# Linear-attention layer and MLP on one core: both tiles of a pair combined in one visit, the second in two of the MLP's banks

## The chip, the core and the metric

The kernel runs on one core of one Trainium2 chip. A core has five engines that each run their own list of instructions in order: TensorE (PE, matrix products; its weight loads are listed as PEld), VectorE (DVE), ScalarE (ACT), GpSimd (POOL) and SyncE (SP, which here issues most transfers). Semaphores order the lists against each other. Matrix products are written to PSUM, a small memory of eight banks per partition; DVE and ACT read them from there. The metric is the time of one execution on the device in microseconds (us).

## The reference

Input x is 2048 tokens of 576 numbers in bf16. The first half is attention with feature maps and no attention matrix; the second half is an MLP. Both have a residual.

```python
def A(x, wqkv, w_phi, wo):                    # 32 heads of 18
    q, k, v = split(x @ wqkv)
    pq, pk = q @ w_phi, k @ w_phi             # per head, 18 x 18
    phi_q = concat(softmax(pq), softmax(-pq)) # 36 features
    phi_k = concat(softmax(pk), softmax(-pk))
    kv, z = phi_k.T @ v, phi_k.sum(tokens)    # 36 x 18 and 36, per head
    o = (phi_q @ kv) / (phi_q @ z + 1e-6)
    return o @ wo

def B(x, w1, b1, w2, b2):                     # 576 -> 4608 -> 576
    return gelu(layernorm(x) @ w1 + b1) @ w2 + b2

h  = x + A(layernorm(x), ...)
h2 = h + B(layernorm(h), ...)
```

## The kernel before

The 2048 tokens are 16 tiles of 128 (NT = 16), taken in eight pairs of 256 (TB). Tile t belongs to pair p = t // 2.

The prologue normalises x, makes keys and values for all pairs and sums phi_k.T @ v over all tokens into `acc_kv`. It also makes the exponentials of the queries of all pairs, which wait in SBUF. From the masked table `kvm` on, each tile needs only its own queries. Pair 0 is finished there, with steps of its own.

The rest is the MLP, and the attention of the later pairs is threaded through it. `first_block` runs the MLP for pair 0, `second_block` for pair 1, and `double_block` for pairs 2 and 3, then 4 and 5, then 6 and 7.

- `up` (L1129) is the first layer. It has 18 steps, which the text calls pairs of `up`, numbered 0 to 17: in each, 18 matmuls (L1142) fill two banks `ph`, which ACT reads and writes as gelu to a buffer (L1164). The matmuls use 64 of the 128 rows of the array each (64 of 576 inputs at a time), two in turn on the two halves. One pair of tiles gives 256 columns, a double block 512.
- `down` (L1170) is the second layer. A tile's output is two `po` tiles of 288 columns, each the sum of 36 matmuls with all 128 rows (L1186). They are numbered from 0 through the block by k: 144 in a block of one pair, 288 in a double block. DVE adds `hb` (residual and bias, made by POOL at L1175) and writes `ot` (L1190), which SP sends out.

Both take a dictionary `at`: at a given step of `up`, or before a given matmul k of `down`, a piece of the attention is called. All engines are under a manual schedule, so each engine runs its instructions in the order in which the program calls them: where a piece stands in `at` is where it stands on every engine.

The pieces for a pair p are:

- `norm_q(p, i)`: DVE sums one half of the exponentials and takes the reciprocal (`query_sum`, L503 and L504); POOL multiplies them into `padded` (`query_weigh`, L512 and L522).
- `turn_q(p)`: two transposing transfers on SP turn `padded` into `phiT[p]` (L546). Most pairs use the buffer `phit`; pairs 3 and 5 take two of the eleven SBUF buffers called homes. The home of the pair's exponentials is given back here. Homes are taken from the front of a list and given back to its end; the gelu outputs of `up` live in homes too.
- `combine(t)` (L664): `combine_mm` multiplies the tile's queries with `kvm` in eleven matmuls of 57 or 38 columns (L641) into a tile `pn` of two banks; `divide` then divides by the denominators on DVE, in four instructions (L654 twice, L655 twice), into `ob`. `pn_pool` holds one tile, so the matmuls of the next `combine` wait until the last `divide` has read it.
- `leave(p)`: `combine` of the odd tile, then `turn(p)`, a transposing transfer of `ob` on SP (L672).
- `enter(p)`: the products with `wo` (L689), the residual (L698), the second layernorm and its transposes (L735), ahead of the MLP for that pair.

After the prologue PSUM is divided so: two banks for `pn_pool`, and six for the pool `acc`, from which `ph`, `po` and the products `pa` of `enter` take one bank at a time:

```python
    acc = ctx.enter_context(
        tc.tile_pool(name="acc", bufs=6, space=bass.MemoryType.PSUM, reuse_waits="tile")
    )
```

`combine` of the even tile is called by itself, before `leave` of the pair:

| Block | even tiles (`combine`) | odd tiles (`leave`) |
|---|---|---|
| first, `down` | tile 2 at 0, tile 4 at 84 | pair 1 at 12, pair 2 at 118 |
| second, `up` | tile 6 at step 10 | pair 3 at step 12 |
| second, `down` | tile 8 at 98, tile 10 at 122 | pair 4 at 110, pair 5 at 136 |
| double (pairs 2 and 3), `down` | tile 12 at 110, tile 14 at 190 | pair 6 at 130, pair 7 at 210 |

Of the kernel before, what the change touches and what calls it, by code (L numbers as in the profile page):

```python
# [8 lines left out]
P = 128  # L9
BF16 = mybir.dt.bfloat16  # L10
FP32 = mybir.dt.float32
# [16 lines left out]
VW = DH + 1  # L28
# [15 lines left out]
def kernel(  # L44
# [39 lines left out]
    def take(key):  # L84
        taken[key] = vacant.pop(0)
        return homes[taken[key]][:, :]

    def leave_home(key):
        vacant.append(taken.pop(key))
# [3 lines left out]
    kvm = persist.tile([P, KW, WV], BF16, name="kvm", tag="kvm")  # L93
# [11 lines left out]
    pn_pool = ctx.enter_context(  # L105
        tc.tile_pool(name="pn_pool", bufs=1, space=bass.MemoryType.PSUM, reuse_waits="tile")
    )
    psA = ctx.enter_context(ExitStack())
    two = psA.enter_context(
        tc.tile_pool(name="two", bufs=3, space=bass.MemoryType.PSUM, reuse_waits="tile")  # L110
    )
# [26 lines left out]
    def region(at, n):  # L138
        return shared[:, at : at + n]
# [314 lines left out]
    phik, phiq, phiT = {}, {}, {}  # L454
# [44 lines left out]
    def query_sum(p, i):  # L499
        if p not in rescaled:  # L500
            rescaled[p] = small.tile([P, 2, 2 * NH], FP32, name="rq", tag="rq", bufs=3)
        sk = small.tile([P, 2, NH], FP32, name="sk", tag="sk", bufs=6)
        nc.vector.tensor_reduce(sk[:, :, :], part_of(phiq[p], i), AX.X, ALU.add)  # L503
        nc.vector.reciprocal(rescaled[p][:, :, i * NH : (i + 1) * NH], sk[:, :, :])  # L504

    def query_weigh(p, part, a, eng):
        src = phiq[p][:, a, :].rearrange("p (h f) -> p h f", f=DH)
        rk = rescaled[p][:, a, :]
        n = 2 * WH
        g0 = part * 5  # L510
        hs = slice(g0 * n, (g0 + 5) * n)
        eng.tensor_tensor(  # L512
            padded[:, a, g0 * P : (g0 + 5) * P].rearrange("p (g k) -> p g k", k=P)[
                :, :, 0:STEP
            ].rearrange("p g (h f) -> p g h f", f=DH),
            src[:, hs, :].rearrange("p (g h) f -> p g h f", h=n),
            rk[:, hs].rearrange("p (g h o) -> p g h o", h=n, o=1).to_broadcast([P, 5, n, DH]),
            ALU.mult,
        )
        if part:  # L520
            m = 2 * COUNT[-1]
            eng.tensor_tensor(  # L522
                padded[:, a, KW * P - m * DH : KW * P].rearrange("p (h f) -> p h f", f=DH),
                src[:, 2 * NH - m :, :],
                rk[:, 2 * NH - m :].rearrange("p (h o) -> p h o", o=1).to_broadcast([P, m, DH]),
                ALU.mult,
            )

    def norm_q(p, i):
        query_sum(p, i)  # L530
        for a in range(2):
            query_weigh(p, i, a, pool)

    def turn_q(p):
        if p == 0:
            whole = region(4 * PW, 2 * KW * P).rearrange("p (a w k) -> p a w k", a=2, k=P)
            phiT[p] = [whole[:, a, :, :] for a in range(2)]
        elif p in (3, 5):
            phiT[p] = [
                take(("phiT", p, a))[:, 0 : KW * P].rearrange("p (w k) -> p w k", k=P)  # L540
                for a in range(2)
            ]
        else:
            phiT[p] = [phit[:, a, :, :] for a in range(2)]
        for a in range(2):
            nc.sync.dma_start_transpose(phiT[p][a], padded[:, a, :])  # L546
        leave_home(("phiq", p))

    left = list(range(NT))

# [78 lines left out]
    products = {}  # L629

    def combine_mm(t, part=None, home=None):
        p, a = divmod(t, 2)
        if not part:
            products[t] = (home or pn_pool).tile(
                [P, 2, 512], FP32, name="pn", tag="two" if home else "pn"
            )
        pn = products[t]
        for w in range(*((0, KW) if part is None else BANKS[part])):
            b = w // 6
            at, n = (w - BANKS[b][0]) * WV, COUNT[w] * VW  # L640
            nc.tensor.matmul(  # L641
                pn[:, b, at : at + n], phiT[p][a][:, w, :], kvm[:, w, 0:n],
                start=True, stop=True,
            )
        if part != 0 and ("phiT", p, a) in taken:
            leave_home(("phiT", p, a))

    def divide(t):
        o = ob[t // 2 % 2][:, :, t % 2, :].rearrange("p c (e h) -> p c e h", e=2)
        rec = small.tile([P, NH], FP32, name="rec", tag="rec")  # L650
        for w0, w1_ in BANKS:
            h0, h1 = FIRST[w0], min(NH, w1_ * WH)
            pv = products[t][:, w0 // 6, 0 : (h1 - h0) * VW].rearrange("p (h v) -> p h v", v=VW)
            nc.vector.reciprocal(rec[:, h0:h1], pv[:, :, DH])  # L654
            nc.vector.tensor_tensor(  # L655
                o[:, :, :, h0:h1],
                pv[:, :, 0:DH].rearrange("p h (c e) -> p c e h", e=2),
                rec[:, h0:h1].rearrange("p (u v h) -> p u v h", u=1, v=1).to_broadcast(
                    [P, KC, 2, h1 - h0]
                ),  # L660
                ALU.mult,
            )

    def combine(t):  # L664
        combine_mm(t)
        divide(t)

    def out_rows(p):
        return ob[p % 2][:, :, :, :].rearrange("p c a k -> p (c a k)")
# [1 line left out]
    def turn(p):  # L671
        nc.sync.dma_start_transpose(oT[p % 2][:, :, :], out_rows(p))  # L672
# [41 lines left out]
    def residual(p, banks):  # L714
        for i in range(2):
            residual_mm(p, i, banks())
            for a in range(2):
                residual_add(p, i, a)
            for a in range(2):
                residual_stats(p, i, a)  # L720
                if i:
                    second(2 * p + a)

    def rescale(t, half):
        mv, rs = moved[t]
        normalise(ln2[t % 2][:, :, half, :], chunks(t), mv, rs, 0)
# [7 lines left out]
    def turn2(t):  # L734
        nc.sync.dma_start_transpose(place2(t), rows2(t))  # L735

    def turn2_mm(t, home=None):
        transposes(("2", t), rows2(t), home)
# [18 lines left out]
    def close_weights():  # L757
# [362 lines left out]
    acc = ctx.enter_context(  # L1120
        tc.tile_pool(name="acc", bufs=6, space=bass.MemoryType.PSUM, reuse_waits="tile")
    )
# [75 lines left out]
    def enter(a):  # L1198
        residual(a, two_banks)
        for t in (2 * a, 2 * a + 1):  # L1200
            rescale(t, 0)
            rescale(t, 1)
            turn2(t)

    def leave(p, following=None):
        combine(2 * p + 1)
        if following:
            turn_q(following)
        turn(p)
# [4 lines left out]
    def first_block():  # L1214
        rise = up(0, 1, {}, 1)
        turn2_mm(1, pn_pool)
        next(rise)
        for n in range(2):
            load_w2(1, n)
        for part in range(2):  # L1220
            turn2_ev(1, part, dve)
        for q in (1, 2):
            for i in range(2):
                norm_q(q, i)
            if q == 1:
                turn_q(q)
                for n in range(2, 6):
                    load_w2(1, n)
        down(0, 1, next(rise), {
            0: lambda: combine(2), 12: lambda: (leave(1), turn_q(2)), 66: lambda: enter(1),  # L1230
            84: lambda: combine(4),
            96: lambda: norm_q(3, 0), 118: lambda: leave(2),
        })

    def second_block():
        hidden = next(up(1, 1, {
            3: lambda: (norm_q(3, 1), turn_q(3)),
            6: lambda: norm_q(4, 0),
            8: lambda: (norm_q(4, 1), turn_q(4)),
            10: lambda: combine(6),  # L1240
            12: lambda: leave(3),
            14: lambda: norm_q(5, 0),
            16: lambda: (norm_q(5, 1), turn_q(5)),
        }))
        enter(2)
        down(1, 1, hidden, {
            44: lambda: enter(3), 98: lambda: combine(8), 110: lambda: leave(4),
            122: lambda: combine(10), 136: lambda: leave(5),
        })

    def double_block(p):
        rises, falls = {}, {}
        if p == 2:
            rises = {
                3: lambda: norm_q(6, 0), 6: lambda: (norm_q(6, 1), turn_q(6)),
                12: lambda: norm_q(7, 0), 15: lambda: norm_q(7, 1),
            }
            falls = {
                110: lambda: combine(12), 130: lambda: leave(6, 7),
                190: lambda: combine(14), 210: lambda: leave(7),  # L1260
            }
        hidden = next(up(p, 2, rises))
        if p + 2 < NS:
            enter(p + 2)
            enter(p + 3)
        down(p, 2, hidden, falls)
# [36 lines left out]
```

## Time and profile before

| What | Before |
|---|---|
| median of 3 runs | 393.16 us (392.96 to 394.19) |
| the profiled execution's own time | 392.96 us |
| its span | 391.2 us |
| PE / DVE / ACT / POOL busy | 98% / 42% / 42% / 33% of the span |
| `po` matmuls (L1186) | 144.0 us busy, 1151 recorded |
| `ph` matmuls (L1142) | 141.5 us busy, 1638 |
| `divide`: L654 and L655 | 8.1 us in 32 and 14.6 us in 32 instructions |

The span is the time from the first to the last recorded work of the profiled execution; its own time is a little longer. In the lines below, the chain in order of time has the start, the length, and what the time went to; "issue" is time in which an engine waited for nothing that the profile shows. A row of the timeline has the start, the length, the engine, the line and the operation, output and inputs, and in brackets how long the engine stood idle before and what ended that. Rows that say x11 take eleven instructions together. Matmuls overlap, so the length of a group in the timeline is a little more than its share of the chain.

### The profile page before, as it was taken

What the parts mean: (1) busy time and instruction counts of PE and PEld (TensorE: products, weight loads), DVE (VectorE), ACT (ScalarE), POOL (GpSimd) and SP (SyncE); (2) the same over time, 40 slices, a digit from 0 to 9 for tenths busy, and PEclk for the clock granted to TensorE, in tenths of its full rate; (3) what the DMA queues carried; (4) which work ended last, traced back from release to release, by engine and by line L of the source; (5) the groups of instructions that cost most, each with busy time, mean ns of one, the idle gap of its engine ahead of it and who ended that gap; (6) DMA issues with size and microseconds to landing.
All of it is one profiled execution on the core that took longest, in us unless ns stands there. A gap on an engine that the chain in (4) does not pass through costs nothing.

```text
span 391.2 us, 10255 instructions
## 1 busy us (share of the span) xinstructions
PE 383.5 (98%) x4492; PEld 266.6 (68%) x4493; DVE 164.2 (42%) x367; ACT 163.5 (42%) x290; POOL 128.2 (33%) x167
## 2 busy tenths in 40 slices
PE   8899999999999999999999999999999999999997
PEld 4687777779878887744457887444677764447773
DVE  6988893694259478680029431000480000000100
ACT  4978878688401850046650000666300016661000
POOL 8999998215514563144003111000031110000120
PEclk9999999999999999999999999999999999999999
DMA  8999749999455466532004532000041000000000
GB/s 224 197 169 168 173 107 202 230 315 251 159 106 122 76 107 134 107 78 45 0 2 63 124 72 47 17 1 2 2 104 48 17 17 0 2 2 0 17 28 19
DMA packets 76108, 34.76 MB, mean 89 GB/s; under 512 B 63026, under 2 KB 73536, under 8 KB 76064
## 3 DMA queue, kind: packets, MB, share of 16 engines
q1 hardware_dynamic: 75376, 32.47, 39.9%
q0 software_dynamic: 400, 1.35, 1.3%
q8 instruction: 35, 0.57, 0.6%
q10 hardware_dynamic: 288, 0.30, 0.2%
q14 instruction: 9, 0.07, 0.1%
HBM read 16.53 MB, written 2.36 MB: 48 GB/s over the span
## 4 chain that ended last, share of the span: by engine, by line
PE 94%; DVE 4%; POOL 1%; issue 1%; POOLq 0%
PE po L1186 36%; PE ph L1142 36%; PE pk L426 7%; PE pa L689 5%; PE pv L426 4%; PE acc_kv L559 2%; PE pn L641 1%; PE pw L250 1%; DVE st L293 1%; POOL wv L174 1%; DVE ob L655 0%; PE pW L396 0%; DVE shared L260 0%; PE pT L338 0%; DVE shared L314 0%
## 5 line engine op out<-in xcount | busy, mean ns | idle before, releaser
L1164 ACT ACTIVATE home<-ph,b1col 128x512 bf16<-128x512 f32 (+1 forms) x180 | 98.5, 598 | 170.7 <-PE ph L1142 167.4
L1186 PE MATMUL po<-w,home 128*128 128x288 bf16 (+2 forms) x1151 | 144.0, 286 | 0.1
L1142 PE MATMUL ph<-shared,w 64*128 64x512 bf16 (+2 forms) x1638 | 141.5, 331 | 0.1
L1186 PEld LDWEIGHTS <-home 128*128 128x128 bf16 x1152 | 109.0, 98 | 31.7 <-issue 1.6
L1142 PEld LDWEIGHTS <-w 64*128 64x128 bf16 x1638 | 80.1, 94 | 60.2 <-issue 1.2
L1190 DVE TENSOR_TENSOR ot<-po,hb 128x288 bf16<-128x288 f32 (+2 forms) x32 | 14.5, 454 | 108.3 <-PE po L1186 104.8
L1175 POOL TENSOR_TENSOR hb<-xh,b2bc 128x576 f32<-128x576 bf16 x16 | 20.4, 1272 | 103.6 <-DVE ot L1190 94.3
L426 PEld LDWEIGHTS <-home 64*128 64x128 bf16 x864 | 41.9, 94 | 10.6 <-issue 0.9
L512 POOL TENSOR_TENSOR padded<-home,rq 128x540 bf16<-128x540 bf16 x32 | 34.8, 1102 | 35.2 <-DVE rq L504 14.5
L256 POOL TENSOR_TENSOR rs<-va,mhalf 128x1 f32<-128x1 f32 x16 | 8.8, 550 | 108.3 <-DVE va L254 108.3
L698 DVE TENSOR_TENSOR xh<-pa,xh 128x288 bf16<-128x288 f32 x32 | 13.2, 450 | 73.7 <-PE pa L689 73.7
L483 POOL TENSOR_TENSOR phik<-phik,rk 128x576 bf16<-128x576 bf16 x32 | 36.3, 1160 | 1.1 <-DVE rk L479 0.8
L477 DVE TENSOR_REDUCE sk<-phik 128x64 f32<-128x1152 bf16 x16 | 21.2, 1327 | 4.8 <-ACT phik L448 4.8
L448 ACT ACTIVATE home<-pk 128x576 bf16<-128x576 f32 x32 | 18.9, 650 | 6.7 <-PE pk L426 5.5
L503 DVE TENSOR_REDUCE sk<-home 128x64 f32<-128x1152 bf16 x16 | 21.0, 1313 | 0.0
L426 PE MATMUL pv<-wv,home 64*128 64x288 bf16 x288 | 20.8, 283 | 0.1
L448 ACT ACTIVATE phik<-pk 128x576 bf16<-128x576 f32 x32 | 18.7, 652 | 3.1 <-PE pk L426 3.1
L426 PE MATMUL pk<-wqp,home 64*128 64x288 bf16 x288 | 19.8, 283 | 0.2 <-ACT home L448 0.2
L426 PE MATMUL pk<-shared,home 64*128 64x288 bf16 x288 | 19.8, 283 | 0.0
L689 PE MATMUL pa<-wo,shared 64*128 64x288 bf16 x288 | 18.8, 283 | 0.0
L654 DVE RECIPROCAL rec<-pn 128x18 f32<-128x18 f32 (+1 forms) x32 | 8.1, 252 | 24.6 <-PE pn L641 24.6
L689 PEld LDWEIGHTS <-shared 64*128 64x128 bf16 x288 | 13.8, 94 | 4.4 <-issue 0.5
(78 smaller groups left out, 209.9 us busy)
## 6 DMA issues: line engine op xcount, KB each, us to landing
w<-in_B_w_dram SPq DMA_DIRECT2D x21, 432.0 KB, 7.5
out_dram<-ot SPq DMA_DIRECT2D x15, 144.0 KB, 1.9
xh<-in_A_x_dram SPq DMA_DIRECT2D x3, 576.0 KB, 6.8
wo<-in_A_wo_dram SPq DMA_DIRECT2D x4, 324.0 KB, 7.0
w<-in_B_w_dram POOLq DMA_DIRECT2D x3, 432.0 KB, 10.3
wv<-in_A_wqkv_dram SPq DMA_DIRECT2D x2, 324.0 KB, 9.0
w<-in_A_wqkv_dram SPq DMA_DIRECT2D x4, 157.5 KB, 8.8
wqp<-wqp SPq DMA_DIRECT2D x2, 288.0 KB, 4.0
```

Of the source, the lines that this page charges most:

```text
L426: nc.tensor.matmul(dst[:, a, 0:HALF], lhs[rows, c, :], w[rows, slot, i * HALF : (i + 1) * HALF], start=(n == 0), stop=(n == KC - 1),)
L448: nc.scalar.activation(rows[:, :, i * HH : (i + 1) * HH, s, :], flight[key, p, i][:, :, 0:HALF].rearrange("p a (h f) -> p a h f", f=DH), A ...
L477: nc.vector.tensor_reduce(sk[:, :, :], part_of(dst, i), AX.X, ALU.add)
L483: eng.tensor_tensor(part, part, flight["r" + key, p, i][:, a, :].rearrange("p (h o) -> p h o", o=1).to_broadcast([P, NH, DH]), ALU.mult,)
L503: nc.vector.tensor_reduce(sk[:, :, :], part_of(phiq[p], i), AX.X, ALU.add)
L512: eng.tensor_tensor(padded[:, a, g0 * P : (g0 + 5) * P].rearrange("p (g k) -> p g k", k=P)[:, :, 0:STEP].rearrange("p g (h f) -> p g h f", ...
L689: nc.tensor.matmul(pa[a], oT[p % 2][rows, c, :], wo[rows, c, cs], start=(c == 0), stop=(c == KC - 1),)
L1142: nc.tensor.matmul(ph[half][:, lo:hi], w1[p_ // 9][rows, c, p_ % 9 * P : (p_ % 9 + 1) * P], ln2T[rows, c, base + lo : base + hi], start=(c ...
L1164: nc.scalar.activation(hidden(m), ph[half][:, 0:width], AF.Gelu_apprx_tanh, bias=b1col[:, m : m + 1], scale=1.0,)
L1175: nc.gpsimd.tensor_tensor(hb[:, :], xh[:, t, :], b2bc[:, :], ALU.add)
L1186: nc.tensor.matmul(po[:, :], hidden(m)[:, i_ * P : (i_ + 1) * P], w2[m // 18][:, m % 18, cs], start=(j == 0), stop=(j == NM - 1),)
L1190: nc.vector.tensor_tensor(ot[:, cs], po[:, :], hb[:, cs], ALU.add)
```

## The change

`leave(p)` now does both tiles: the products of the even tile into `pn_pool`'s tile, those of the odd tile into two tiles of one bank each from `acc` (`acc_banks`), and then both divisions, the even tile's first. The separate calls of `combine` are gone, and some of the places in `at` are moved: the visit of pair 1 is at matmul 2, of pair 2 at 112, of pair 4 at 104; pairs 3, 5, 6 and 7 stay where `leave` was. `products[t]` becomes a list of two banks, so that the code of both kinds of tile is the same. The home of a pair's exponentials is given back at the end of `norm_q(p, 1)`, when POOL has been told to weigh them, and no longer in `turn_q` (pair 0 excepted).

```diff
@@ norm_q
         query_sum(p, i)
         for a in range(2):
             query_weigh(p, i, a, pool)
+        if i:
+            leave_home(("phiq", p))
@@ turn_q
             nc.sync.dma_start_transpose(phiT[p][a], padded[:, a, :])
-        leave_home(("phiq", p))
+        if p == 0:
+            leave_home(("phiq", p))
@@ combine_mm
         if not part:
-            products[t] = (home or pn_pool).tile(
-                [P, 2, 512], FP32, name="pn", tag="two" if home else "pn"
-            )
+            if home is acc_banks:
+                products[t] = home()
+            else:
+                whole = (home or pn_pool).tile(
+                    [P, 2, 512], FP32, name="pn", tag="two" if home else "pn"
+                )
+                products[t] = [whole[:, b, :] for b in range(2)]
...
-                pn[:, b, at : at + n], phiT[p][a][:, w, :], kvm[:, w, 0:n],
+                pn[b][:, at : at + n], phiT[p][a][:, w, :], kvm[:, w, 0:n],
...
-    def combine(t):
-        combine_mm(t)
-        divide(t)
+    def acc_banks():
+        return [
+            acc.tile([P, 512], FP32, name="pn", tag="acc")[:, :] for _ in range(2)
+        ]
...
     def leave(p, following=None):
-        combine(2 * p + 1)
+        combine_mm(2 * p)
+        combine_mm(2 * p + 1, None, acc_banks)
+        divide(2 * p)
+        divide(2 * p + 1)
         if following:
             turn_q(following)
         turn(p)
@@ first_block
-            0: lambda: combine(2), 12: lambda: (leave(1), turn_q(2)), 66: lambda: enter(1),
-            84: lambda: combine(4),
-            96: lambda: norm_q(3, 0), 118: lambda: leave(2),
+            2: lambda: (leave(1), turn_q(2)), 66: lambda: enter(1),
+            96: lambda: norm_q(3, 0), 112: lambda: leave(2),
@@ second_block
-            10: lambda: combine(6),
             12: lambda: leave(3),
...
-            44: lambda: enter(3), 98: lambda: combine(8), 110: lambda: leave(4),
-            122: lambda: combine(10), 136: lambda: leave(5),
+            44: lambda: enter(3), 104: lambda: leave(4), 136: lambda: leave(5),
@@ double_block
-                110: lambda: combine(12), 130: lambda: leave(6, 7),
-                190: lambda: combine(14), 210: lambda: leave(7),
+                130: lambda: leave(6, 7), 210: lambda: leave(7),
```

More of the change, by code (lines that the diff above doesn't have):

```diff
@@ L652, in divide @@
             h0, h1 = FIRST[w0], min(NH, w1_ * WH)
-            pv = products[t][:, w0 // 6, 0 : (h1 - h0) * VW].rearrange("p (h v) -> p h v", v=VW)
+            pv = products[t][w0 // 6][:, 0 : (h1 - h0) * VW].rearrange("p (h v) -> p h v", v=VW)
             nc.vector.reciprocal(rec[:, h0:h1], pv[:, :, DH])
```

## The prediction

> **What bounds the kernel now.** I read the page first: engine shares, clock, shares of the chain that ended last.
>
> ```profile
> span 391.2 us, 10255 instructions
> PE 383.5 (98%) x4492; PEld 266.6 (68%) x4493; DVE 164.2 (42%) x367; ACT 163.5 (42%) x290; POOL 128.2 (33%) x167
> ...
> PEclk9999999999999999999999999999999999999999
> ...
> PE 94%; DVE 4%; POOL 1%; issue 1%; POOLq 0%
> ```
>
> TensorE is busy 98% of the span at the full granted clock and makes 94% of the chain; so a change is worth what it takes off TensorE's own stream. Next I read the chain in order of time around each visit of the combining products (L641). The first answer holds the visits of the first block's second layer, at matmuls 0, 12, 84 and 118:
>
> ```profile
> 102.38 0.42 PE pn L641 x11
> 102.79 1.48 PE po L1186 x12
> 104.27 0.11 issue
> 104.38 0.47 PE pn L641 x11
> 104.85 6.62 PE po L1186 x54
> ...
> 116.10 0.31 PE pn L641 x11
> ...
> 120.58 0.31 PE pn L641 x11
> ```
>
> The second holds the second block: tiles 6 and 7 among the pairs of `up`, tiles 8 to 11 in `down` at 98, 110, 122 and 136:
>
> ```profile
> 134.01 0.41 PE pn L641 x11
> 134.42 2.07 PE ph L1142 x36
> 136.49 0.41 PE pn L641 x11
> 136.91 6.00 PE ph L1142 x108
> ...
> 159.64 0.31 PE pn L641 x11
> 159.95 1.48 PE po L1186 x12
> 161.43 0.11 issue
> 161.54 0.47 PE pn L641 x11
> 162.01 1.48 PE po L1186 x12
> 163.49 0.12 issue
> 163.60 0.47 PE pn L641 x11
> 164.07 1.72 PE po L1186 x14
> 165.79 0.34 PE pn L641 x11
> ```
>
> The third holds the double block, tiles 12 to 15, first and last of four equal visits:
>
> ```profile
> 220.18 0.31 PE pn L641 x11
> ...
> 233.37 0.31 PE pn L641 x11
> ```
>
> An undisturbed visit between `po` matmuls costs 0.31 us. Three cost 0.58: 0.11 or 0.12 of idle time, then 0.47, because the weight load could not run ahead of the wait. What they wait for is in the timeline, a waiting pair of tiles first and an unhurried one behind it:
>
> ```profile
> 103.82 0.42 DVE L655 TENSOR_TENSOR ob<-pn,rec 128x252 bf16<-128x252 f32 x1
> 104.35 0.39 PEld L641 LDWEIGHTS <-phit 128*128 128x128 bf16 x11 [0.39 <-issue]
> ...
> 160.97 0.42 DVE L655 TENSOR_TENSOR ob<-pn,rec 128x252 bf16<-128x252 f32 x1
> 161.51 0.39 PEld L641 LDWEIGHTS <-phit 128*128 128x128 bf16 x11 [0.39 <-issue]
> ...
> 221.51 0.42 DVE L655 TENSOR_TENSOR ob<-pn,rec 128x252 bf16<-128x252 f32 x1
> 222.66 0.48 PEld L641 LDWEIGHTS <-phit 128*128 128x128 bf16 x11
> ```
>
> The weight load starts 0.11 and 0.12 us behind the end of the previous tile's last division (104.24, 161.39): with one `pn` tile, the next tile's products wait until the last one is divided. Twelve `po` matmuls (1.48) are too short a distance. At 222.66 the division had ended 0.73 us before, and nothing waited.
>
> **The change, part by part.**
>
> *The distance-12 waits go.* The odd tile's products no longer need the pool's only tile. Matmuls 0 and 12 become one visit at 2: 0.42+0.11+0.47 = 1.00 becomes 0.31+0.31, and the step from the row-split `ph` to `po`, which no row shows alone; its bounds are 0 and the 0.11 by which a `pn` visit next to `ph` (0.42) exceeds one next to `po` (0.31). I take 0.08, as the exit from `ph` is only part of that row: saved 0.30, at least 0.27, at most 0.38. Visits 98, 110, 122, 136 become 104 and 136: 0.31+0.58+0.59+0.34 = 1.82 becomes 1.24: saved 0.58.
>
> *Visits without a wait merge at no gain.* Matmuls 84 and 118 (now 112), and 110, 130, 190, 210 (now 130, 210): six at 0.31 become three at 0.62, since the second eleven matmuls still run. Saved 0, between -0.05 and +0.05 by the rounding of the rows.
>
> *In `up`, one of two excursions goes.* Leaving `ph` and coming back costs more than a visit in `po`: 0.41 against 0.31, and the 36 `ph` matmuls between the two visits took 2.07 where 6.00/108 gives 2.00. Two excursions (0.41 twice, 0.07 beside) become one with 0.31 more: saved 0.10 to 0.17; I take 0.14.
>
> *A new wait: two of six banks are out while DVE divides.* In the second layer that is free: a `po` tile takes 36 x 6.62/54 = 4.4 us and needs one bank, and the four divisions of a tile take 1.32 (next fence, 118.79 to 120.11), so a pair takes about 2.64. The even tile is divided first. In `up` it is tight:
>
> ```profile
> 118.79 0.27 DVE L654 RECIPROCAL rec<-pn 128x18 f32<-128x18 f32 x1
> ...
> 120.11 1.34 DVE L503 TENSOR_REDUCE sk<-home 128x64 f32<-128x1152 bf16 x1
> ...
> 133.94 0.48 PE L641 MATMUL pn<-kvm,home 128*128 128x57 bf16 x11
> ...
> 134.46 0.27 DVE L654 RECIPROCAL rec<-pn 128x18 f32<-128x18 f32 x1 [4.44 <-PE pn L641]
> 134.77 0.50 DVE L655 TENSOR_TENSOR ob<-pn,rec 128x324 bf16<-128x324 f32 x1
> ```
>
> As the changed kernel is built, tile 7's two banks, before pair 12, are pair 9's; they go on to the first half of pair 14 and the first half of pair 15. Count from the visit's first matmul. The first division starts at 0.52 (133.94 to 134.46); tile 7's begins at 0.52+1.32 = 1.84; its first bank is read by 1.84+0.81 = 2.65 (134.46 to 135.27), and TensorE sees that 0.12 later, at 2.77; the second bank at 0.52+2.64+0.12 = 3.28. TensorE is through tile 6 at 0.31, tile 7 at 0.72, and two pairs of 18 x 6.00/108 = 1.00 bring it to pair 14 at 2.72, its weight load a little earlier. It stalls some 0.05 to 0.12, and as in the waits above the halted weight load adds 0.16 (0.47 less 0.31): 0.21 to 0.28. If the load is not caught, 0. I take 0.23, as the sum decides for a late load by little. Pair 15 comes at 3.9, behind its bank's 3.28: no second stall. DVE was idle 4.44 us before the division (row 134.46), so nothing is queued ahead of it.
>
> *Waits on ScalarE.* Tile 3's products now need two banks of `ph` pairs 15 and 16, whose activations are the fifth- and fourth-last of this row:
>
> ```profile
> 85.75 17.48 ACT L1164 ACTIVATE home<-ph,b1col 128x256 bf16<-128x256 f32 x36 [0.41 <-PE ph L1142]
> ...
> 137.25 3.86 SPq L546 DMA_TRANSPOSE phit<-padded  x2
> ...
> 141.20 1.31 SPq L672 DMA_TRANSPOSE shared<-ob  x1
> 141.77 1.10 POOL L512 TENSOR_TENSOR padded<-home,rq 128x540 bf16<-128x540 bf16 x1 [3.22 <-DMA phit<-padded]
> ```
>
> At 17.48/36 = 0.486 each they end at 103.23 - 4 x 0.486 = 101.29 and at 101.77; tile 3's products start at about 103. Cost 0.
>
> *What is queued behind the longer divisions.* On DVE the `ot` addition (L1190) after a visit comes up to 1.3 us later; its bank is not asked for again for several `po` tiles, and `hb` on POOL has 4.4 us. In `up` the query sums of pair 5 stand behind it and come up to 1.3 later, but POOL's weighing, their reader, stood 3.22 us for a DMA until 141.77; cost 0, and if that cover went, 1.3 on POOL, which no TensorE row near it waits for. On SP, `turn(3)` waits for the last division, now about 133.94 + 2 x 1.00 + 3.28 = 139.2; it already stood behind the transposes of `turn_q(4)` (row 137.25) until 141.20. In `down` of the first block the visit at 112 lies 32 matmuls ahead of `up`, whose pair 1 takes the first of its banks: it comes 0.62 + 32 x 6.62/54 + 1.00 = 5.5 behind the visit's start, and the bank is free at 2.77, or with a whole query sum (1.34) ahead of the divisions at 4.1. Cost 0.
>
> *Queries' buffers given up when weighed.* `leave_home` moves ahead of the two `take`s in `turn_q`, but freed homes go to the end of the list; as built, ACT, POOL and SP have the same instructions, homes and order as before. So the transposes that a visit issues (`turn`, `turn_q`) pass no other transfer in SP's queue; those of the first visit, ten matmuls earlier, only start sooner. Cost and gain 0.
>
> **Sum.** 0.30+0.58+0+0.14-0.23 = 0.79 us saved; with the ends, 0.27+0.58-0.05+0.10-0.28 = 0.62 to 0.38+0.58+0.05+0.17 = 1.18. The profiled execution took 392.96 (span 391.2 and 1.76 around it) and would take 392.17. The median of the runs stands 0.20 above it; from there, 393.16 - 0.79 = 392.37. I give 392.3, between the two.
>
> **Rivals.**
> - *All the waits go and no bank is missed*: 1.0 to 1.18 saved, 392.0 to 392.15. For it: TensorE reaches pair 14 within 0.1 us of the bank's release, and one late weight load decides. Against it: by the row 134.46 it is the division that comes last.
> - *The bank wait eats the gain*: pair 14 waits for the whole visit's divisions, 0.56 after it is ready (3.28 less 2.72), with 0.16 for the load 0.72, and pair 15 and the activations behind it fall out of step for a pair's half (0.5): 1.22 lost against 1.02 saved, 393.4, no change. For it: six banks hold only three pairs. Against: each bank has its own wait. The Trainium skill (Perfetto Trace Analysis, section Optimization Strategy) reads a gap that recurs on the busiest engine as a possible shortage of PSUM for the next tile. By that rule the loan of two banks in `up` makes a new shortage, and the time would be 393.4 where the rows of the divisions give 392.3; the trace agrees with it for the gaps of 0.11, which end when the one `pn` tile is divided, and shows none yet for the banks of `up`.
> - *Slower*: the divisions of the visit in `up` start late. Each us for which DVE is held there goes straight to TensorE at pair 14; the gain is gone from 0.79 us of delay, and the time is 0.3% above the median from 1.97. With one query sum ahead (1.34) it is 392.37 + 1.34 = 393.7, with two 395.0. For it: such sums are called four pairs before and two pairs behind the visit. Against: DVE had idled 4.44 us when the visit came two pairs earlier (row 134.46).
>
> **How the numbers follow.** Likeliest 0.62 (391.8 to 392.6), no bank missed 0.18, eaten 0.10, slower 0.10. Of 393.16, 0.3% is 1.18 us, about what a measurement of this kernel can tell from no change: only the top of the first rival and the runs' own spread reach it, so faster 0.22, within 0.68, slower 0.10. For 8 in 10 I take 391.6 (the first rival, less the 0.4 or so by which a median of other runs may lie lower: the lowest run shown is 0.2 under it) to 393.4 (the gain eaten).
>
> **What would show it.** Seven visits of `pn` x22 at 0.62 and no issue rows before them right the first term; a gap before the row-split matmuls 36 places behind the visit in `up` (some 0.1, with the weight load named, released by L655's `ob`) rights the stall, none refutes it. `ph` and `po` pitches (6.00/108, 0.123) must be unchanged. I am wrong if gaps stand before `po`, or if several pairs behind the visit wait on ACT or DVE.

## The result, and the profile after

| | median, us | lowest to highest |
|---|---|---|
| before, 9 runs | 392.96 | 392.85 to 394.19 |
| after, 9 runs | 392.19 | 391.86 to 392.69 |

The ratio is 0.9976, with a 95% interval of 0.9965 to 0.9986: a gain of 0.77 us by the medians, which is inside the 0.3% that the prediction called no change. The profiled execution of after is the slowest of its nine, 392.69. Its page is hardly to be told from that of before:

```profile
span 391.0 us, 10251 instructions
...
PE 383.6 (98%) x4492; PEld 267.2 (68%) x4493; DVE 163.5 (42%) x367; ACT 163.7 (42%) x290; POOL 128.2 (33%) x167
...
PE 94%; DVE 4%; POOL 1%; issue 1%; POOLq 0%
```

A change of 0.8 in 391 us is read where it is made. This is the chain of after, in order of time (start, length, what), from the first `ph` of the first block to the first `ph` of the block of pairs 4 and 5:

```profile
85.26 17.89 PE ph L1150 x342
103.15 0.35 PE po L1194 x2
103.50 0.62 PE pn L648 x22
...
111.97 2.31 PE pa L697 x36
...
120.02 0.62 PE pn L648 x22
...
124.56 11.90 PE ph L1150 x216
136.46 0.73 PE pn L648 x22
137.19 6.00 PE ph L1150 x108
143.19 2.21 PE pa L697 x36
...
160.66 0.62 PE pn L648 x22
...
165.21 0.62 PE pn L648 x22
...
166.82 35.07 PE ph L1150 x324
...
222.33 0.62 PE pn L648 x22
...
242.94 17.15 PE ph L1150 x157
```

From 85.26 on there is no "issue" row and no other engine left in it: TensorE never stands. All seven visits are one row of 22 matmuls, six of 0.62 and the one in `up` of 0.73. The same chain of before has these marks. The visits between them stand in the prediction, and with them two further marks: the products of `enter(1)` begin at 111.47 (104.85 and 6.62) and those behind `up` at 142.91 (136.91 and 6.00).

```profile
84.50 17.88 PE ph L1142 x342
...
124.08 9.93 PE ph L1142 x180
...
167.12 35.07 PE ph L1142 x324
...
243.24 16.94 PE ph L1142 x155
```

Call the way from the first mark to the last *the stretch*. It holds every place that the change touches, and it can be split at the marks that both chains have. Two of the experiments below stand beside it already; each number is a difference of two starts.

| Section | before | after | `banks_only` | `apart` |
|---|---|---|---|---|
| first block, to the products of `enter(1)` | 26.97 | 26.71 | 26.70 | 26.71 |
| on to `up` of the second block | 12.61 | 12.59 | 12.60 | 12.60 |
| `up` of the second block | 18.83 | 18.63 | 18.83 | 18.83 |
| `down` of the second block | 24.21 | 23.63 | 23.63 | 23.62 |
| double block of pairs 2 and 3 | 76.12 | 76.12 | 76.13 | 76.13 |
| the stretch | 158.74 | 157.68 | 157.89 | 157.89 |

The stretch became 1.06 us shorter, not 0.77. Five of the kernels measured here have a stretch of 157.68 or 157.69: after, `homes_before`, `odd_first`, `late_one` and `late_sum`. Their medians lie 0.77, 1.37, 1.24, 1.09 and 0.93 below those of before beside them, 1.08 on average. So the change is worth about 1.06, and the 0.77 lies within the scatter of medians (by the interval of the ratio the gain is 0.55 to 1.38): the prologue alone puts the first `ph` anywhere from 84.50 to 86.23 in the profiles taken. Part of the scatter goes with the granted clock: of the 25 runs of before beside the `between` kernels below, the seven with a mean of 0.996 took 394.11 to 397.01 us, the others at most 393.54. For that reason the experiments are read by the stretch and only then by the time.

### The profile page after: what moved, and what is told of

Its sections match the earlier page's. It is cut to its first block, busy times and chain, and to the rows that moved or that the text cites. A ratio compares the mean times of both kernels' runs of the same rounds, so it can differ in the third digit from the quotient of the medians.

```text
span 391.0 us, 10251 instructions
## 1 busy us (share of the span) xinstructions
PE 383.6 (98%) x4492; PEld 267.2 (68%) x4493; DVE 163.5 (42%) x367; ACT 163.7 (42%) x290; POOL 128.2 (33%) x167
## 4 chain that ended last, share of the span: by engine, by line
PE 94%; DVE 4%; POOL 1%; issue 1%; POOLq 0%
PE po L1194 36%; PE ph L1150 36%; PE pk L426 7%; PE pa L697 5%; PE pv L426 4%; PE acc_kv L562 2%; PE pw L250 1%; PE pn L648 1%; DVE st L293 1%; POOL wv L174 1%; DVE ob L662 0%; PE pW L396 0%; DVE shared L260 0%; PE pT L338 0%; DVE shared L314 0%
```

## The experiments

The diffs are against after, that of `apart` against before.

**Waits or merging: `banks_only`.** The second tile gets its banks from `acc`, and the tiles are called where before called them.

```diff
+    def combine(t):
+        combine_mm(t)
+        divide(t)
@@ leave
-        combine_mm(2 * p)
         combine_mm(2 * p + 1, None, acc_banks)
-        divide(2 * p)
         divide(2 * p + 1)
@@ first_block; second_block and double_block likewise as before
-            2: lambda: (leave(1), turn_q(2)), 66: lambda: enter(1),
-            96: lambda: norm_q(3, 0), 112: lambda: leave(2),
+            0: lambda: combine(2), 12: lambda: (leave(1), turn_q(2)), 66: lambda: enter(1),
+            84: lambda: combine(4),
+            96: lambda: norm_q(3, 0), 118: lambda: leave(2),
```

> The odd tile's products go to two of the MLP's banks, but even and odd tile keep the places that they had before (no merging). The stretch is taken from the first ph matmul of the first block to the first ph matmul of the block of pairs 4 and 5: 158.74 us in the profile of before, 157.68 in that of after. Theory (the gain is the waits for the one pn tile): the gaps of 0.11, 0.11 and 0.12 are gone and those visits cost 0.31 like the others, 0.84 less than before, so the stretch is 157.9 +- 0.1; the two visits among the ph matmuls still cost 0.41 each. Rival (the gain is the merging, fewer excursions): the three gaps stay in some form and the stretch is 158.4 to 158.7.

Measured: 392.46 us against 393.53, ratio 0.9975 (0.9964 to 0.9985), stretch 157.89. Its chain:

```profile
104.70 0.31 PE pn L648 x11
...
134.16 0.41 PE pn L648 x11
...
161.58 0.31 PE pn L648 x11
...
163.37 0.31 PE pn L648 x11
```

The three visits that had 0.11 or 0.12 of idle time and 0.47 are 0.31 with nothing ahead. So 0.85 of the 1.06 is the waits, and the other 0.21 (157.89 less 157.68) is merging; by the table 0.20 of that lies in `up`, where 0.41 still stands twice (134.16, and again at 136.65).

**Distance instead of banks: `apart`.** The kernel of before, with the places of `combine` moved so that 20 `po` matmuls lie between the tiles of a pair; no bank is lent.

```diff
-            0: lambda: combine(2), 12: lambda: (leave(1), turn_q(2)), 66: lambda: enter(1),
+            0: lambda: combine(2), 20: lambda: (leave(1), turn_q(2)), 66: lambda: enter(1),
...
-            44: lambda: enter(3), 98: lambda: combine(8), 110: lambda: leave(4),
-            122: lambda: combine(10), 136: lambda: leave(5),
+            44: lambda: enter(3), 76: lambda: combine(8), 96: lambda: leave(4),
+            116: lambda: combine(10), 136: lambda: leave(5),
```

> The kernel before with its one pn tile, only with visits moved apart: tiles 2 and 3 at 0 and 20, tiles 8, 9, 10, 11 at 76, 96, 116 and 136. Theory (a visit waits while the last tile is divided, and twelve po matmuls are too short for that): at twenty matmuls nothing waits, the gaps go without any bank, stretch 157.9 +- 0.1. Rival (the gaps belong to the order of the weight loads or to the fetching of instructions, and only the other banks cure them): gaps of about 0.1 remain before the odd tiles' products, stretch 158.5 to 158.8.

Measured: 392.73 us, ratio 0.9986 (0.9968 to 1.0004), stretch 157.89. Its chain where the waits had been:

```profile
106.00 0.31 PE pn L641 x11
...
160.18 0.31 PE pn L641 x11
...
162.94 0.31 PE pn L641 x11
```

The cause of the waits is shown from the other side: with one `pn` tile and 20 matmuls between, the division is over in time and the whole 0.85 is had without any bank. The time by itself cannot be told from before, since 12 runs scatter from 392.2 to 396.58; the reading rests on the chain.

**Merging without the banks: `merged_one_tile`.** Both tiles in one visit, both in the one `pn` tile.

```diff
-        combine_mm(2 * p)
-        combine_mm(2 * p + 1, None, acc_banks)
-        divide(2 * p)
-        divide(2 * p + 1)
+        for t in (2 * p, 2 * p + 1):
+            combine_mm(t)
+            divide(t)
```

> The merging alone: both tiles in one visit, at the places of after, but both in the one pn tile, so the odd tile's products stand until the even tile is divided. Theory: per visit the division ends 0.52 + 1.41 = 1.93 us behind the first matmul, TensorE goes on 0.12 later and then needs 0.47: 2.5 in place of 0.62, seven times 1.9 = 13.3 more than after; stretch 171.0, time about 405.5. Rival (the merged visit hides the division behind its own products): the cost is under 0.5 per visit, stretch below 161.

Measured: 406.65 us, ratio 1.0342 (1.0322 to 1.0362), stretch 170.99. The first visit in its chain:

```profile
103.50 0.32 PE pn L648 x11
...
103.84 0.28 DVE rec L661
...
104.83 0.43 DVE ob L662
105.26 0.14 issue
105.40 0.47 PE pn L648 x11
```

A visit costs 1.9 us more than in after ((170.99 - 157.68) / 7): TensorE stands through the division and pays 0.47 for the next tile's products. In after the two lent banks take all of this off the path.

**The queries' buffers: `homes_before`.** After, with the home of the exponentials given back in `turn_q` again.

```diff
-        if i:
-            leave_home(("phiq", p))
...
-        if p == 0:
-            leave_home(("phiq", p))
+        leave_home(("phiq", p))
```

> After, with only the buffers of the queries given back where before gave them back (in turn_q). All engines have the instructions, waits and order of after, so the stretch is 157.7 +- 0.1 and the time that of after, 392.2 +- 0.3; how much the start of the first ph matmul differs (85.26 in the profile of after, 84.50 in that of before) shows how much the prologue varies by itself. Rival (the earlier return matters): the stretch moves by more than 0.2.

Measured: 392.16 us, ratio 0.9969 (0.9958 to 0.9979), stretch 157.69. In the trace, the instructions and waits of every engine are those of after. This part of the change is worth nothing, and the run is a second sample of the same program: its profile's first `ph` starts at 84.75, that of after at 85.26.

**Which tile is divided first: `odd_first`.** If a wait for the lent banks were hidden somewhere, giving them back first would shorten the stretch.

```diff
-        divide(2 * p)
         divide(2 * p + 1)
+        divide(2 * p)
```

> After with the odd tile divided before the even one, so that the MLP's two banks come back 1.3 us earlier. If pair 14 of up does not wait in after (its ph matmuls kept 6.00 us for 108), nothing is to be had here: stretch 157.7 +- 0.1. Rival (a hidden wait of up to 0.2 us remains there): stretch 157.5.

Measured: 392.24 us, ratio 0.9976 (0.9965 to 0.9988), stretch 157.68, that of after. The order is worth nothing, so after pays nothing in time for its banks.

**DVE busy ahead of the visit in `up`: `late_one` and `late_sum`.** These were to price the prediction's rival "slower". `late_one` puts one reciprocal whose result is not used ahead of the divisions of pair 3; `late_sum` puts there the query sum that otherwise follows at step 14 (`leave` calls what it is given ahead of the two divisions).

```diff
@@ late_one, in leave
+        if p == 3:
+            idle = small.tile([P, 2, NH], FP32, name="idle", tag="idle", bufs=1)
+            nc.vector.reciprocal(
+                idle[:, :, :],
+                wmask[:, 0:1].rearrange("p (a h) -> p a h", a=1).to_broadcast([P, 2, NH]),
+            )
         divide(2 * p)
@@ late_sum, in second_block
-            12: lambda: leave(3),
-            14: lambda: norm_q(5, 0),
+            12: lambda: leave(3, None, lambda: norm_q(5, 0)),
```

> After with one more reciprocal of 128x64 (0.55 us, its result unused) ahead of the divisions in the visit of pair 3 in up. Theory (the release of the bank stands right at pair 14, without slack): the first bank is free 0.55 later, pair 14 stands 0.4 to 0.55 and its halted weight load adds up to 0.16: the 108 ph matmuls behind the visit take 6.4 to 6.7 in place of 6.00, and the stretch is 158.1 to 158.4. Rival (slack of more than half a microsecond that the arithmetic missed): 6.00, stretch 157.7.

> After with the query sum and reciprocal of pair 5's first half (1.34 and 0.55 us, called two pairs later in after) ahead of the divisions of the visit in up. Theory: a late division is paid one to one at pair 14, 1.8 us plus up to 0.16; the 108 ph matmuls take 7.7 to 8.0, stretch 159.4 to 159.7, time 0.8 us over before. Rival (pair 14 is covered by other work, or ScalarE makes the time good again): less than half of it, stretch below 158.6.

Measured: 392.39 us, ratio 0.9978 (0.9968 to 0.9988), and 392.55 us, ratio 0.9982 (0.9965 to 0.9998); both stretches 157.69. Both expectations were missed, and the timelines say why. The first division of the visit, in `late_one`:

```profile
136.16 0.27 DVE L661 RECIPROCAL rec<-pn 128x18 f32<-128x18 f32 x1 [6.00 <-PE pn L648]
```

and in `late_sum`:

```profile
136.77 0.27 DVE L661 RECIPROCAL rec<-pn 128x18 f32<-128x18 f32 x1 [4.61 <-PE pn L648]
```

In after the idle time in these brackets is 6.41. What was put ahead needs nothing of the visit, so DVE ran it in that idle time and still waited for the products. The two runs delayed nothing, and measured the cover instead: a whole query sum fits in front of the divisions and costs nothing.

**DVE busy between the two divisions: `between_small`, `between_one`, `between_sum`.** The same kinds of work, put where DVE has no idle time: behind the even tile's division and ahead of the odd tile's, which frees the banks of `acc`. An operation on 128x1, the unused reciprocal of 128x64, or the query sum, which is only moved. The first of them:

```diff
         divide(2 * p)
+        if p == 3:
+            idle = small.tile([P, 1], FP32, name="idle", tag="idle", bufs=1)
+            nc.vector.tensor_scalar(idle[:, :], wmask[:, 0:1], 1.0, EPS, ALU.mult, ALU.add)
         divide(2 * p + 1)
```

> After with a tensor_scalar of 128x1 (about 0.15 us, result unused) between the two divisions of the visit in up, where DVE cannot run it ahead of the visit. In after the weight load of pair 14 starts 139.08, 0.05 behind the end of the bank's last read (139.03), and the matmuls keep their pitch: no slack left. Theory (release and arrival of pair 14 coincide): the load and the matmuls behind it come about 0.1 to 0.15 later, plus up to 0.16 if a halted weight load costs what it costs in the visits of before; the 108 ph matmuls take 6.1 to 6.3. Rival (slack): 6.00.

> The same with a reciprocal of 128x64 (0.55 us) between the two divisions. Theory: pair 14 stands about 0.45 to 0.55, plus up to 0.16; 108 ph matmuls 6.45 to 6.7, stretch 158.1 to 158.4. Rival (slack of half a microsecond): 6.00 and 157.7.

> The same with the query sum and the reciprocal of pair 5's first half (1.34 and 0.55 us) between the two divisions, taken from two pairs later. Theory: a late division is paid one to one at pair 14, about 1.8 us plus up to 0.16, since ScalarE and the later banks cannot give it back; 108 ph matmuls 7.7 to 8.0, stretch 159.4 to 159.7, about 0.9 us slower than before. Rival (TensorE makes some of it good behind pair 14): less than 1.2 of it, stretch below 158.9.

First the same place in after. The divisions and the weight load of pair 14, the first that needs a lent bank (timeline; the last row is that of a window that begins at 139.07):

```profile
136.39 0.80 PE L648 MATMUL pn<-kvm,home 128*128 128x57 bf16 x22
136.91 0.27 DVE L661 RECIPROCAL rec<-pn 128x18 f32<-128x18 f32 x1 [6.41 <-PE pn L648]
...
138.53 0.50 DVE L662 TENSOR_TENSOR ob<-pn,rec 128x324 bf16<-128x324 f32 x1
139.08 0.12 PEld L1150 LDWEIGHTS <-w 64*128 64x128 bf16 x4
```

The bank is read until 139.03, 2.57 after the visit began in the chain (136.46), and the load follows 0.05 later. That load did wait. In narrow windows of the timeline the loads ahead of it start in twos every 0.11 (138.66, 138.77, 138.88), so its turn was 138.99, and it came 0.09 late; in `odd_first` the loads at this place keep their 0.11. But each load starts 0.11 ahead of its own matmul, and the first matmul of pair 14 starts at 139.10, in step with those before it (138.88, 138.99). The wait lay within this lead and cost nothing. Then `between_small`, the visit in the chain, and the division of the lent bank and the load that waits for it in the timeline:

```profile
137.44 0.73 PE pn L648 x22
138.17 6.06 PE ph L1150 x108
```

```profile
139.57 0.49 DVE L662 TENSOR_TENSOR ob<-pn,rec 128x324 bf16<-128x324 f32 x1
...
140.12 1.97 PEld L1150 LDWEIGHTS <-w 64*128 64x128 bf16 x38 [0.16 <-DVE ob L662]
```

`between_one`, in the same two views:

```profile
135.91 0.43 PE pn L648 x11
```

```profile
138.38 0.50 DVE L662 TENSOR_TENSOR ob<-pn,rec 128x324 bf16<-128x324 f32 x1
...
138.93 1.10 PEld L1150 LDWEIGHTS <-w 64*128 64x128 bf16 x22 [0.51 <-DVE ob L662]
```

And `between_sum`, whose visit begins at 136.04 in the chain, in the timeline:

```profile
137.81 1.34 DVE L503 TENSOR_REDUCE sk<-home 128x64 f32<-128x1152 bf16 x1
...
139.90 0.50 DVE L662 TENSOR_TENSOR ob<-pn,rec 128x324 bf16<-128x324 f32 x1
...
140.45 0.09 PEld L1150 LDWEIGHTS <-w 64*128 64x128 bf16 x1 [0.82 <-DVE ob L662]
...
141.06 2.84 PEld L1150 LDWEIGHTS <-w 64*128 64x128 bf16 x53 [0.51 <-DVE ob L662]
```

| | median, us | ratio | bank read until, from the visit's start | `up` | stretch |
|---|---|---|---|---|---|
| after | 392.19 | 0.9976 (0.9965 to 0.9986) | 2.57 | 18.63 | 157.68 |
| `between_small` | 392.26 | 0.9966 (0.9937 to 0.9995) | 2.62 | 18.69 | 157.75 |
| `between_one` | 392.73 | 0.9991 (0.9973 to 1.0008) | 2.97 | 19.03 | 158.10 |
| `between_sum` | 393.64 | 1.0000 (0.9985 to 1.0016) | 4.36 | 20.04 | 159.10 |

A bank 0.05 later costs 0.06, one 0.40 later costs 0.40. The idle load time is some 0.1 more each time (0.16 and 0.51): that is the lead. So in after the bank comes free when all but 0.02 of the lead is used up: there is hardly any slack left, and the matmuls do not stall yet. The 108 `ph` matmuls behind the visit take 6.06 and 6.40, just under the expected 6.1 to 6.3 and 6.45 to 6.7, as a halted load adds nothing of its own. `between_sum` missed its expectation (7.41 against 7.7 to 8.0). It costs 1.41 for a bank that is 1.79 later: as built, its pair 14 takes two banks that pair 12 had, both lent banks go to pair 15, and the wait comes a pair later, in two parts (0.82 and 0.51 of idle weight load). The whole gain is gone: the stretch is 0.36 longer than that of before, and the time is that of before.

**The visit out of `up`: `visit_in_down` and `visit_in_down_88`.** If leaving the row-split matmuls costs, then pair 3's visit belongs into `down`, among `po`. Its `enter(3)` needs the result, so it has to move too: to 66, or to 88.

```diff
-            12: lambda: leave(3),
...
-            44: lambda: enter(3), 104: lambda: leave(4), 136: lambda: leave(5),
+            2: lambda: leave(3), 66: lambda: enter(3), 104: lambda: leave(4), 136: lambda: leave(5),
```

> After with the visit of pair 3 moved from step 12 of up to matmul 2 of the second layer of the same block, and enter(3) from 44 to 66 behind it. Theory (an excursion from the row-split ph matmuls costs 0.10 to 0.18 more than one from po): the visit costs 0.62, stretch 157.5 to 157.6, faster than after by 0.1 to 0.2 us. Rival (enter(3) is now late: its transposes hold up the first ph of the next block): a gap before that block, stretch above 157.8.

> The visit of pair 3 at matmul 2 of the second layer again, but enter(3) at 88 in place of 66, behind the time at which the transpose of pair 3's rows landed (156.1 in the profile with 66, where TensorE stood 2.61 us for it). Theory (the excursion from the row-split matmuls is what the merged visit in up still pays): the 18 pairs of up lose 0.86 and the second layer gains 0.62, so the stretch is 157.68 - 0.24 = 157.4 to 157.5, and this is the fastest of all by 0.2 us. Rival (the work of enter(3) on DVE and its transposes now end too late for the next block): a gap of 0.3 us or more before the first ph of the double block or before the visit at 136, stretch 157.7 or more.

Measured for the first: 396.04 us, ratio 1.0061 (1.0043 to 1.0078), stretch 160.16, so the expectation was missed. `enter(3)` was late, as the rival had it, but the gap stands before its own products and not before the next block. The timeline:

```profile
150.53 0.26 DVE L661 RECIPROCAL rec<-pn 128x18 f32<-128x18 f32 x1
...
153.27 1.27 SPq L680 DMA_TRANSPOSE shared<-ob  x1
...
156.16 1.03 PE L697 MATMUL pa<-wo,shared 64*128 64x288 bf16 x14 [2.61 <-DMA shared<-ob]
```

The divisions of the visit stood behind DVE's work for `enter(2)` until 150.53, with no idle time in brackets; the transfer of `ob` followed at 153.27, and TensorE stood 2.61 us for it. With `enter(3)` at 88, 392.04 us, ratio 0.9970 (0.9960 to 0.9980), stretch 157.51. Its chain:

```profile
123.80 17.79 PE ph L1150 x324
...
144.15 0.62 PE pn L648 x22
144.77 10.54 PE po L1194 x86
155.31 2.31 PE pa L697 x36
```

No gap is left, and `up` without a visit takes 17.79 where after takes 18.63: the visit in `up` costs 0.84, in `down` 0.62. The stretch is the shortest measured, 0.17 below that of after. The times (392.04 and 392.19, each against its own runs of before) do not tell the two apart.

## Why the prediction was right, and which step was not

The forecast of 392.3 (391.6 to 393.4) holds the 392.19, but by two errors that cancel: the sum was 0.79 and the stretch gained 1.06, while the medians happened to differ by 0.77. What took place in the kernel is the first rival, *all the waits go and no bank is missed*, which had 0.18.

- *The distance-12 waits go*, 0.30 and 0.58: measured 0.26 (26.97 to 26.71) and 0.58 (24.21 to 23.63). The first lies just under its lower end of 0.27. Half of what it lacks is the step from `ph` to `po`, which was put at 0.08 and is 0.10 (0.35 for two `po` matmuls that take 0.123 each); the rest is of the size of the rounding of the rows. `banks_only` and `apart` show that the one `pn` tile caused the waits: two banks or eight more matmuls remove them alike.
- *Visits without a wait merge at no gain*, 0: the sections that hold them moved by 0.02 and 0.00.
- *In `up`, one of two excursions goes*, 0.14, at most 0.17: 0.20. By `visit_in_down_88` an excursion costs 0.22 beside its 0.62, so the rows of the prediction caught only part of the way back. The 6.00 for 108 that it took for undisturbed holds part of a way back itself: at the 17.79 for 324 of `visit_in_down_88`, 108 take 5.93.
- *A new wait: two of six banks are out while DVE divides*, -0.23: 0. **This is the term that was mis-sized.** Its times were good: the bank was read until 2.64 after the first matmul of the timeline (139.03 less 136.39), where 2.65 was forecast, and the first matmul of pair 14 came at 2.71 (139.10), where 2.72 was. The load was late too, as forecast, by 0.09. Two figures put on top were wrong. The 0.12 until TensorE sees the end was 0.05 here (139.03 to 139.08), so the load still came 0.02 ahead of the time of its matmul; with 0.12 it would have come 0.05 behind it. And the 0.16 for a halted weight load is not paid by row-split matmuls: in `between_one` the load stood 0.51 and `up` became longer by the delay of the bank alone, 0.40. The prediction had said that the sum decides by little; it fell on the other side, and `odd_first` confirms that nothing is paid.
- *Waits on ScalarE*, *queued behind the longer divisions*, *queries' buffers*: no row of the chain shows another engine, and `homes_before` shows the last to change nothing in what the engines run. The transfer of `ob` was forecast to come only behind the transposes of `turn_q(4)`, and did: 17.23 after the start of `up` (141.79 less 124.56), against 17.12 before (141.20 less 124.08), with no reader on TensorE that waited:

```profile
141.79 1.50 SPq L680 DMA_TRANSPOSE shared<-ob  x1
```

The rival *slower* had its price right and its place wrong. A bank that comes later is paid one for one, within 0.02, from the first hundredths (0.05 for 0.06, 0.40 for 0.40). But a query sum ahead of the visit could not have delayed it, as `late_sum` shows; it takes work between the two divisions. *The bank wait eats the gain* did not happen: in after the matmuls of pairs 14 and 15 kept their step.

Two causes stay open. Why eleven `pn` matmuls behind a halted load take 0.47 and not 0.31, while `ph` matmuls pay nothing extra, was seen but not tried. And what moves the prologue's end by more than a microsecond between profiles of kernels that do not differ there is not shown. The latest, 86.23 in `between_small`, goes with a granted clock of 0.96 over the first 40 us, where before and after had 1.00; but `visit_in_down` had 0.96 there too, and its first `ph` is at 85.43.

## What to carry to other kernels

When two engines hand one buffer back and forth, first ask what else removes the wait: here a longer distance gave 0.85 of the 1.06 us without any new buffer. Before lending banks of a shared pool, set the time at which the last reader is through against the time at which the next writer comes, to the tenth of a microsecond, and tell the writer's load from its matmul, since a late load costs nothing while its lead lasts (0.11 here); work behind which the reader stands counts only if it lies where the reader has no idle time. Where the gain is smaller than the scatter of medians, compare a stretch of the chain between two marks that both kernels have: it repeated to 0.01 us in five kernels whose gains by the medians scattered by 0.6.

## What the runs showed of the hardware that was not expected

How long TensorE takes to see DVE's end depends on what the weight load waits for. Of the lines of the products in before and in after, the instruction counts of TensorE's load queue are these, before first:

```profile
L641 PEldq EVENT_SEMAPHORE  x11: 51/51/51, 69.8 to 232.4; - x11
```

```profile
L648 PEldq EVENT_SEMAPHORE  x4: 51/51/51, 70.6 to 230.4; - x4
```

Eleven loads of before wait on DVE (the `pn` tile) and on a transfer (the transposed queries), and have a semaphore instruction of 51 ns ahead of them for DVE. Where DVE was late, such a load started 0.11 or 0.12 behind DVE's end; a `ph` load that waits on DVE alone started 0.05 behind it. The difference is about that instruction. The change also took seven such instructions out: in after, only four loads of the products wait on DVE as well.

Going from matmuls that use 64 rows to matmuls that use 128 took 0.10 us, alike for `po` (0.35 for two) and for `pn` (0.41 against 0.31); going there and back took 0.22.
